# A fused attention and expert kernel: second batch's loads at another place in the queue, and a new order of its steps

## The chip, the cores and the metric

The kernel runs on one core of one Trainium2 chip. The metric is device time in microseconds (us) of one execution; lower is better. The engines are PE (TensorE matmul; PEld is its weight load), DVE (VectorE), ACT (ScalarE), POOL (GpSimd) and SP (SyncE, which here only issues DMAs). Each engine works through its own instructions in program order and waits where an operand isn't there yet.

## What is computed

Four batches, four heads, 1088 positions of 32 values; everything is float32 outside.

```python
a, b = S1 @ x, S2 @ x                    # two sketches of 8 values, for x = q and x = k
phi(x) = outer(a, b)                     # 64 features
kv = sum_s phi(k)_s v_s ;  z = sum_s phi(k)_s
attn = (phi(q) kv) / (phi(q) z + 1e-6)   # 4352 tokens x 128
h = attn @ w_in                          # 128 -> 2048
P = a0 + a1 h + a2 h^2 + a3 h^3 ;  Q = 1 + |b0||h| + |b1| h^2
out = (P / (Q + 1e-6)) @ w_out           # 2048 -> 128
```

## The kernel before

**Stages.** `keys(b)` makes one batch's k features and sums them with v (transposes L414/L416 on DVE, sketches L434 on PE, copies L439 on ACT, features L442 on DVE, products L453 on PE, L470 keeps the sum). `queries(b)` makes q features and the quotient, in chunks of up to 384 positions: transposes L493; then either "direct" (sketches L515, copies L520/L523, features L527/L530; the first 512 positions of batch 0) or "spread" (sketches L543, copy L548, two stores of the sketch to DRAM, `put`, and three reads of it back in a repeated layout, `get`, then features L551); then products L581, L590 to L597 on DVE, transpose back L603 on PE, and L610 on ACT into `xT`. `unit(i)`, 29 of them, takes blocks of 128 hidden values by 256 or 512 tokens: hidden matmuls L683, evacuation L687, |h| L698, L703/L705, L708, Ln L711, Exp L714, L718/L720 and so on, and output matmuls L779 whose weights are w_out times a0..a3 (`w_part`, L390 to L396). A unit's mode (2, 3 or 4) says how the polynomial is split: mode 3 has three output matmuls per block and two products on DVE; mode 2 has two, and instead a product (L732), an addition (L736 on DVE or L738 on ACT) and a product (L741).

**The order.** The program is a list of 976 steps. `step(...)` makes a step in the order in which the code creates it (that index is the step number used below), `PLACE[number]` is its place in the program, and `run` issues all steps by place. `after` and `behind` serve for an assertion on places alone; what really waits for what follows from the data. `rank`, `slack`, `early`, `rate`, `cost` are left from the planner that made PLACE and have no effect when the kernel is built. `ON_ACT` lists the steps, among those that either engine can do, that go to ACT; the others go to DVE. `FILLS` puts matmuls on idle data (L320) ahead of a place.

**Buffers.** `kq` 3 (k or q of one batch), `v_sb` 1, `a_all`, `b_all`, `sk_d` 2 each, PSUM `h` 2, `out` 2, `att` 2.

**Loads.** All go through SP's queue, except k of batch 0 (step 2) and the two tiny loads of `ab_row` (steps 7, 8, the polynomial's constants), which ACT issues first of all. `load_v` is two DMAs: partitions 0 to 63 and 64 to 127. A product L453 contracts over all 128 partitions, so it reads both; the `after` at L464 named both only for the last part.

Steps around the change:

| step | engine | what |
|---|---|---|
| 3 | ACT | preload of the table set (L293) |
| 9, 11 | SP | the halves of w_in |
| 12, 117 | SP | k and q of batch 1 |
| 115, 116 | SP | v of batch 1, first and second half |
| 13, 14 | SP | the halves of w_out |
| 16, 21 | PE | transpose of the sketch matrices L348; bias matmul L376, which spreads `ab_row` |
| 24 to 33 | ACT or DVE | scaled w_out, two halves for each of five versions |
| 71, 87 | ACT | copies L520 and L548 of batch 0, positions 256 to 512 and 512 to 768 |
| 73, 79 | PE | products L581 of positions 256 to 512 |
| 88, 89; 90 to 92 | SP | stores and reads of the first spread chunk (batch 0, 512 to 768) |
| 93, 98, 99 | DVE, PE, ACT | its features L551, transpose back L603, copy L610 |
| 103, 104; 105 to 107 | SP | stores and reads of the second spread chunk |
| 122, 123 | DVE, PE | features L442 and products L453 of batch 1, first part |
| 133 | DVE | transposes L493 of batch 1's first queries |
| 306; 342, 343 | PE; ACT, DVE | first hidden matmul (unit 0); steps of unit 2 (L720, L732) |

Of the kernel before, what the change touches and what calls it, by code (L numbers as in the profile page):

```python
# [20 lines left out]
def kernel(  # L21
# [16 lines left out]
    R = S1.shape[0]  # L38
# [6 lines left out]
    NT = 8  # L45
# [79 lines left out]
    def d_four(n, ptr):  # L125
# [14 lines left out]
    LOADS = 1.3  # L140
    LATER = 4.5
# [4 lines left out]
    GET_SLACK = 0.8  # L146
# [6 lines left out]
    MODES = '43242333333243333233444244434'  # L153
# [12 lines left out]
        0, 3, 1, 39, 4, 5, 6, 2, 20, 19, 9, 28, 25, 11, 18, 7, 8, 12, 16, 15, 13, 42, 43, 76, 57, 72, 56,  # L166
        95, 96, 65, 58, 77, 73, 75, 10, 24, 14, 23, 31, 37, 21, 22, 32, 40, 33, 35, 36, 46, 34, 38, 41, 50,
        44, 48, 49, 51, 53, 17, 29, 26, 30, 54, 55, 60, 62, 67, 68, 69, 45, 52, 66, 61, 70, 71, 78, 85, 91,
        115, 121, 86, 87, 93, 94, 124, 125, 47, 59, 63, 64, 79, 80, 81, 90, 126, 131, 138, 143, 144, 149,
        150, 84, 97, 104, 112, 107, 113, 128, 161, 196, 214, 215, 217, 222, 234, 237, 106, 114, 27, 83, 82,  # L170
        110, 111, 120, 146, 127, 137, 145, 152, 98, 100, 108, 172, 198, 102, 155, 156, 159, 160, 171, 178,
        175, 213, 223, 224, 231, 233, 238, 239, 174, 185, 189, 190, 205, 218, 206, 210, 250, 252, 257, 263,
        272, 283, 284, 165, 201, 202, 211, 212, 227, 261, 228, 262, 279, 280, 301, 316, 330, 346, 298, 311,
        334, 268, 318, 299, 359, 360, 361, 381, 357, 358, 366, 382, 331, 332, 342, 384, 386, 288, 295, 309,
        312, 310, 338, 336, 340, 380, 403, 405, 407, 426, 427, 428, 282, 321, 322, 335, 326, 343, 344, 337,
        388, 394, 408, 411, 429, 458, 459, 300, 374, 385, 396, 397, 400, 436, 399, 437, 445, 456, 466, 471,
        478, 481, 469, 505, 542, 440, 470, 482, 496, 504, 520, 587, 495, 545, 562, 590, 558, 571, 594, 602,
        613, 467, 474, 480, 497, 487, 537, 543, 501, 606, 616, 621, 623, 631, 634, 637, 477, 525, 552, 554,
        553, 563, 611, 609, 647, 659, 675, 677, 682, 692, 693, 568, 575, 577, 585, 584, 684, 586, 610, 685,
        698, 735, 738, 747, 757, 772, 74, 88, 92, 101, 103, 109, 119, 122, 129, 141, 135, 133, 134, 142, 89,  # L180
        105, 116, 117, 132, 139, 140, 157, 123, 173, 181, 184, 270, 264, 99, 136, 147, 148, 154, 162, 163,
        176, 153, 164, 167, 183, 203, 200, 118, 130, 151, 166, 169, 179, 180, 187, 188, 216, 245, 240, 207,
        293, 302, 398, 369, 313, 303, 158, 170, 177, 186, 168, 182, 192, 193, 197, 209, 225, 247, 191, 204,
        219, 251, 269, 305, 241, 296, 333, 278, 194, 199, 220, 221, 195, 208, 226, 232, 235, 243, 256, 266,
        248, 290, 304, 319, 323, 294, 291, 392, 383, 414, 422, 391, 230, 242, 229, 236, 244, 246, 254, 259,
        274, 277, 292, 324, 258, 339, 353, 307, 347, 348, 368, 350, 376, 418, 404, 433, 453, 506, 486, 488,
        541, 249, 253, 255, 260, 265, 267, 273, 281, 289, 315, 328, 354, 271, 371, 379, 417, 349, 364, 413,
        416, 377, 483, 412, 449, 275, 276, 287, 297, 285, 286, 308, 317, 329, 351, 367, 372, 378, 395, 424,
        508, 421, 415, 393, 420, 419, 461, 432, 473, 306, 314, 345, 355, 320, 327, 356, 365, 389, 401, 410,
        431, 425, 441, 447, 512, 489, 490, 513, 515, 556, 485, 491, 465, 529, 538, 536, 535, 534, 532, 530,  # L190
        531, 533, 352, 362, 363, 370, 373, 375, 406, 409, 430, 438, 448, 463, 387, 500, 510, 576, 588, 589,
        511, 549, 547, 517, 526, 527, 390, 402, 325, 341, 423, 434, 439, 444, 452, 462, 479, 507, 457, 499,
        524, 540, 548, 523, 555, 550, 559, 573, 600, 716, 746, 727, 612, 435, 443, 451, 455, 442, 446, 468,
        476, 484, 493, 544, 561, 567, 578, 560, 632, 665, 619, 628, 620, 582, 583, 618, 629, 625, 603, 460,
        472, 464, 475, 450, 454, 498, 521, 546, 564, 566, 579, 503, 595, 626, 580, 591, 581, 641, 593, 636,
        696, 681, 688, 494, 514, 492, 502, 509, 518, 522, 551, 569, 597, 605, 615, 519, 633, 644, 650, 642,
        630, 624, 658, 635, 657, 651, 652, 708, 718, 743, 744, 748, 715, 717, 726, 745, 528, 565, 516, 539,
        557, 570, 599, 604, 607, 617, 627, 639, 596, 649, 668, 706, 725, 689, 753, 671, 729, 730, 719, 775,
        572, 574, 601, 614, 592, 598, 622, 646, 661, 663, 672, 687, 643, 701, 711, 709, 723, 691, 731, 713,
        710, 732, 728, 739, 608, 640, 638, 648, 645, 653, 655, 669, 678, 683, 700, 704, 654, 667, 676, 724,  # L200
        754, 769, 755, 776, 795, 793, 786, 787, 849, 844, 855, 664, 670, 656, 662, 660, 666, 679, 686, 694,
        707, 721, 741, 736, 751, 760, 833, 835, 802, 794, 749, 784, 779, 768, 780, 695, 697, 673, 674, 680,
        690, 702, 712, 734, 750, 765, 767, 763, 788, 791, 832, 818, 817, 799, 778, 785, 800, 801, 819, 841,
        859, 858, 852, 854, 853, 842, 850, 845, 699, 703, 705, 720, 714, 722, 737, 756, 761, 773, 782, 797,
        803, 814, 862, 866, 820, 836, 816, 828, 811, 821, 812, 871, 831, 867, 740, 759, 752, 758, 733, 742,
        762, 766, 789, 805, 806, 813, 838, 847, 827, 822, 829, 863, 843, 869, 896, 868, 890, 870, 877, 889,
        764, 771, 770, 774, 790, 798, 809, 810, 826, 864, 879, 898, 840, 872, 876, 894, 904, 891, 911, 908,
        914, 954, 915, 937, 953, 777, 781, 783, 796, 808, 815, 830, 839, 851, 865, 825, 875, 883, 886, 885,
        922, 909, 905, 804, 807, 792, 823, 824, 837, 860, 861, 880, 895, 899, 906, 892, 893, 924, 913, 926,
        910, 923, 921, 936, 941, 939, 940, 938, 834, 846, 848, 857, 873, 874, 884, 888, 900, 912, 929, 949,  # L210
        931, 934, 925, 927, 933, 946, 965, 950, 878, 881, 887, 897, 901, 907, 916, 928, 951, 955, 942, 943,
        957, 963, 902, 903, 919, 920, 932, 944, 945, 952, 930, 959, 967, 956, 962, 968, 856, 882, 917, 918,
        935, 947, 948, 958, 960, 969, 961, 964, 966, 970, 971, 975, 972, 973, 974,
    )
    ON_ACT = (
        26, 27, 28, 29, 31, 33, 328, 342, 379, 454, 478, 502, 535, 612, 636, 669, 693, 717, 744, 876, 914,
        932, 946, 951, 960,
    )
    FILLS = {8: 15, 14: 4}
# [53 lines left out]
    def load_k(b, buf, rank, after=(), early=0.0, slack=0.3, behind=None, rate=250, eng=SP):  # L273
        return [dma(lambda: buf.t, flat(k, b), rank, 0.557, after, [buf], eng=eng, rate=rate, early=early, slack=slack, behind=behind)]
# [11 lines left out]
    def load_s(i, rank, eng):  # L286
        s_in = (S1, S2)[i]
        return dma(s_raw[i * R:(i + 1) * R], s_in, rank, 0.001, eng=eng, cost=0.4, slack=S_SLACK[i])

    s_l = [load_s(0, -206, SP), load_s(1, -205.9, SP)]  # L290
# [11 lines left out]
    def load_w(x, rank):  # L302
        c = x * 1024
        w_l[x] = dma(w_in_sb[:, c:c + 1024], moe_w_in[:, c:c + 1024], rank, 0.524, early=LATER, rate=440, slack=0.3, behind=v0_l[1])
# [5 lines left out]
    k1_l = load_k(1, k1, K1L_RANK, early=LATER, slack=0.3, behind=v0_l[1], rate=350)  # L310
# [95 lines left out]
    def keys(b, kb, vb, k_l, v_l, rank, parts, wide, early=0.0):  # L406
# [16 lines left out]
        for x, (t0, t1) in enumerate(parts):  # L423
# [40 lines left out]
            last = step(PE, 0.265 * n + 0.07, products, r, after=[ft] + (v_l if t1 > NT else v_l[:1]), uses=[k_p, vb, kv], behind=last)  # L464
# [349 lines left out]
    for b in range(1, B):  # L814
        kb, vb, qb = k1 if b == 1 else Buf("kq"), Buf("v_sb"), Buf("kq")
        base = where(b * S)
        gate = wo_l if b == 1 else q_done[b - 1][-1:]
        kl = k1_l if b == 1 else load_k(b, kb, base - 14, gate, slack=1.0)
        vl = load_v(b, vb, LOADS - 0.01 if b == 1 else base - 13.9, gate, slack=V_SLACK)
        ql = dma(lambda qb=qb: qb.t, flat(q, b), LOADS if b == 1 else base - 13.8, 0.557, gate, [qb], rate=250, slack=V_SLACK)  # L820
        keys(b, kb, vb, kl, vl, max(K1_RANK, base - K_LEAD), ((0, 3), (3, 6), (6, 9)), False, LATE)
        for c0 in range(0, S, QN):
            queries(b, qb, ql, c0, min(c0 + QN, S), max(0.5, where(b * S + c0) - Q_LEAD), "spread")
# [34 lines left out]
```

## Time and profile before

| | us |
|---|---|
| median of 3 runs | 269.05 (268.74 to 269.28) |
| the profiled execution | 268.98 |
| its span | 267.2 |
| PE busy | 257.3 (96%) |
| DVE busy | 252.7 (95%) |
| ACT busy | 248.2 (93%) |
| POOL busy | 2.7 (1%) |
| DMA moved | 20.13 MB, mean 75 GB/s |

Times inside the profile count from the start of the span; some 1.8 us of the execution lie around it. Busy time is the union of an engine's instructions. SPq and ACTq are the engines' DMA issues, a "releaser" is what the profile takes to have ended a wait, inferred from semaphores; where the named engine had long been done, it was another.

### The profile page before, as it was taken

Reading aid. Unit: us, or ns where it says so; the run is one execution under the profiler, and the core shown is the slowest. Engines: PE = TensorE matmul, PEld = TensorE weight load, DVE = VectorE, ACT = ScalarE, POOL = GpSimd, SP = SyncE. Lnnn points to the kernel's source line nnn. Section 1 sums busy time; section 2 is a strip of 40 time slices with the busy share of each in tenths; the row PEclk is TensorE's granted clock in tenths of the full one; section 3 lists DMA queues with packets and bytes.
Section 4 is the critical chain, followed back from the end, with each engine's and each line's share of the span. In section 5 each row is a group of like instructions: output and inputs, shape, how many; then the busy total and the mean of one; then the engine's idle time right before and its main releaser. Section 6 shows DMA issues by size and latency. Waiting matters only on the chain.

```text
span 267.2 us, 4218 instructions
## 1 busy us (share of the span) xinstructions
PE 257.3 (96%) x1660; PEld 140.9 (53%) x1660; DVE 252.7 (95%) x294; ACT 248.2 (93%) x208; POOL 2.7 (1%) x25
## 2 busy tenths in 40 slices
PE   8989699999999999999999999999999999999993
PEld 5767545554545455444534445454544466465782
DVE  3989789999999999999999999999999999999994
ACT  1699699999999999999999999999999999999990
POOL 4000000000000000000000000000000000000000
PEclk9999999999999999999999999999999999999999
DMA  7954433660024825300135515000022000013013
GB/s 204 313 226 132 119 98 103 166 207 0 2 56 101 168 55 151 121 0 11 36 70 105 150 40 132 12 2 0 0 29 39 2 10 0 0 27 45 0 27 54
DMA packets 29063, 20.13 MB, mean 75 GB/s; under 512 B 19316, under 2 KB 24948, under 8 KB 29044
## 3 DMA queue, kind: packets, MB, share of 16 engines
q1 hardware_dynamic: 28352, 19.24, 28.4%
q10 hardware_dynamic: 692, 0.62, 0.8%
q8 instruction: 13, 0.21, 0.3%
q14 instruction: 6, 0.05, 0.1%
HBM read 16.65 MB, written 3.21 MB: 74 GB/s over the span
## 4 chain that ended last, share of the span: by engine, by line
PE 32%; DVE 29%; ACT 25%; issue 11%; DMA 1%; SPq 0%; DVEq 0%; ACTq 0%
PE h_ps L683 16%; ACT ln L711 7%; PE out_ps L779 6%; ACT t L687 6%; DVE t L726 5%; ACT t L714 5%; DVE t L723 5%; ACT t L720 4%; DVE t L708 4%; DVE t L698 3%; DVE t L729 3%; PE att_ps L453 3%; DVE t L703 2%; DVE t L744 2%; PE att_ps L581 2%
## 5 line engine op out<-in xcount | busy, mean ns | idle before, releaser
L683 PE MATMUL h_ps<-xT,w_in_sb 128*128 128x512 f32 (+1 forms) x320 | 128.3, 534 | 0.4
L779 PE MATMUL out_ps<-t,w_out 128*128 128x512 bf16 (+1 forms) x501 | 101.3, 345 | 0.3 <-DVE t L726 0.2
L683 PEld LDWEIGHTS h_ps<-xT,w_in_sb 128*128 128x128 f32 x320 | 58.7, 190 | 42.4 <-issue 32.1
L779 PEld LDWEIGHTS <-w_out 128*128 128x128 bf16 x501 | 47.6, 98 | 51.3 <-issue 19.8
L687 ACT CAST t<-h_ps 128x1024 bf16<-128x1024 f32 (+1 forms) x69 | 69.2, 1027 | 0.7 <-PE h_ps L683 0.6
L711 ACT ACTIVATE ln<-t 128x3072 f32<-128x3072 bf16 (+4 forms) x29 | 65.0, 2240 | 0.1
L714 ACT ACTIVATE t<-ln 128x3072 bf16<-128x3072 f32 (+4 forms) x29 | 64.7, 2231 | 0.3
L723 DVE TENSOR_TENSOR t<-t,t 128x3072 bf16<-128x3072 bf16 (+4 forms) x29 | 40.4, 1395 | 0.0
L708 DVE TENSOR_TENSOR t<-t,t 128x3072 bf16<-128x3072 bf16 (+4 forms) x29 | 40.3, 1393 | 0.0
L720 ACT ACTIVATE t<-t,a_sb 128x3072 bf16<-128x3072 bf16 (+3 forms) x15 | 38.3, 2552 | 0.1
L726 DVE TENSOR_TENSOR t<-t,t 128x3072 bf16<-128x3072 bf16 (+4 forms) x24 | 33.3, 1392 | 0.0
L703 DVE TENSOR_SCALAR t<-t,b_abs 128x3072 bf16<-128x3072 bf16 (+2 forms) x25 | 23.8, 951 | 0.1
L698 DVE TENSOR_SCALAR t<-t 128x3072 uint16<-128x3072 uint16 (+4 forms) x29 | 22.4, 775 | 0.9 <-ACT t L687 0.9
L729 DVE TENSOR_TENSOR t<-t,t 128x3072 bf16<-128x3072 bf16 (+2 forms) x14 | 22.1, 1575 | 0.0
L581 PEld LDWEIGHTS att_ps<-kvz,a_all 128*64 128x64 f32 x288 | 9.5, 137 | 6.7 <-issue 3.7
L581 PE MATMUL att_ps<-kvz,a_all 128*64 128x66 f32 x288 | 11.3, 226 | 0.6 <-DVE a_all L527 0.5
L744 DVE TENSOR_TENSOR t<-t,t 128x1024 bf16<-128x1024 bf16 (+3 forms) x10 | 11.1, 1115 | 0.0
L453 PE MATMUL att_ps<-v_sb,k_p 128*64 128x64 f32 x216 | 8.0, 225 | 2.5 <-DVE t L708 2.5
L453 PEld LDWEIGHTS att_ps<-v_sb,k_p 128*64 128x64 f32 x216 | 7.0, 137 | 6.2 <-DVE t L708 2.8
L551 DVE TENSOR_TENSOR a_all<-a_all,b_all 128x768 f32<-128x768 f32 (+2 forms) x11 | 9.6, 877 | 0.0
L732 DVE TENSOR_TENSOR t<-t,t 128x3072 bf16<-128x3072 bf16 (+2 forms) x5 | 7.2, 1432 | 2.4 <-ACT t L720 2.4
L442 DVE TENSOR_TENSOR k_p<-att_ps,b_sk 128x768 f32<-128x768 f32 x9 | 8.6, 951 | 0.3 <-ACT b_sk L439 0.3
(74 smaller groups left out, 136.8 us busy)
## 6 DMA issues: line engine op xcount, KB each, us to landing
a_all<-sk_d SPq DMA_DIRECT2D x6, 384.0 KB
b_all<-sk_d SPq DMA_DIRECT2D x12, 192.0 KB
kq<-in_k_dram SPq DMA_DIRECT2D x3, 544.0 KB
kq<-in_q_dram SPq DMA_DIRECT2D x3, 544.0 KB
a_all<-sk_d SPq DMA_DIRECT2D x4, 320.0 KB
b_all<-sk_d SPq DMA_DIRECT2D x8, 160.0 KB
v_sb<-in_v_dram SPq DMA_DIRECT2D x4, 288.0 KB
v_sb<-in_v_dram SPq DMA_DIRECT2D x4, 256.0 KB
```

The source lines that it names most:

```text
L683: nc.tensor.matmul(h.t[:, cols[x] - cols[x0]:cols[x + 1] - cols[x0]], lhsT=w_in_sb[:, f * 128:(f + 1) * 128], rhs=xT[:, xpos(t0):xpos(t0) ...
L687: nc.scalar.copy(out=hh.t[:, cols[x0]:cols[x1]], in_=h.t[:, 0:cols[x1] - cols[x0]])
L698: nc.vector.tensor_scalar(out=u.t[:, :n].bitcast(U16), in0=hh.t[:, :n].bitcast(U16), scalar1=0x7FFF, scalar2=None, op0=AX.bitwise_and)
L703: nc.vector.tensor_scalar(out=w.t[:, :n], in0=u.t[:, :n], scalar1=ab1, scalar2=ab0, op0=AX.mult, op1=AX.add)
L708: nc.vector.tensor_mul(out=y.t[:, :n], in0=w.t[:, :n], in1=u.t[:, :n])
L711: nc.scalar.activation(out=ln.t[:, :n], in_=y.t[:, :n], func=ACT.Ln, bias=1.0 + 1e-6)
L714: nc.scalar.activation(out=r.t[:, :n], in_=ln.t[:, :n], func=ACT.Exp, scale=-1.0)
L720: nc.scalar.activation(out=p.t[:, :n], in_=hh.t[:, :n], func=ACT.Identity, scale=a3, bias=a2)
L723: nc.vector.tensor_mul(out=s.t[:, :n], in0=hh.t[:, :n], in1=r.t[:, :n])
L726: nc.vector.tensor_mul(out=(hh if mode == 3 else p).t[:, :n], in0=hh.t[:, :n], in1=s.t[:, :n])
L729: nc.vector.tensor_mul(out=hh.t[:, :n], in0=p.t[:, :n], in1=hh.t[:, :n])
L779: nc.tensor.matmul(o[0].t[:, :bl[x][1]], lhsT=w_sb[y_][:, bl[x][2], :], rhs=src.t[:, cols[x]:cols[x + 1]], start=(o[1] == 1), stop=(o[1] = ...
```

## The change

The code, with the long lists cut:

```diff
-    GET_SLACK = 0.8
+    GET_SLACK = 0.9
...
-    MODES = '43242333333243333233444244434'
+    MODES = '43242333333243333233444244424'
...
-        0, 3, 1, 39, 4, 5, 6, 2, 20, 19, 9, 28, 25, 11, 18, 7, 8, 12, 16, 15, 13, 42, 43, 76, 57, 72, 56,
+        0, 1, 2, 7, 5, 6, 10, 3, 4, 43, 11, 45, 39, 16, 14, 8, 9, 17, 23, 18, 55, 13, 15, 34, 97, 53, 96,
...
-        26, 27, 28, 29, 31, 33, 328, 342, 379, 454, 478, 502, 535, 612, 636, 669, 693, 717, 744, 876, 914,
-        932, 946, 951, 960,
+        27, 28, 29, 30, 32, 342, 351, 379, 454, 478, 502, 535, 612, 636, 669, 688, 693, 744, 878, 889, 914,
+        932, 946, 951, 953,
...
-    FILLS = {8: 15, 14: 4}
+    FILLS = {9: 15, 19: 2}
...
-            last = step(PE, 0.265 * n + 0.07, products, r, after=[ft] + (v_l if t1 > NT else v_l[:1]), uses=[k_p, vb, kv], behind=last)
+            last = step(PE, 0.265 * n + 0.07, products, r, after=[ft] + v_l, uses=[k_p, vb, kv], behind=last)
...
-        vl = load_v(b, vb, LOADS - 0.01 if b == 1 else base - 13.9, gate, slack=V_SLACK)
-        ql = dma(lambda qb=qb: qb.t, flat(q, b), LOADS if b == 1 else base - 13.8, 0.557, gate, [qb], rate=250, slack=V_SLACK)
+        vl = load_v(b, vb, LOADS - 0.01 if b == 1 else base - 13.9, gate, slack=3.0 if b == 1 else V_SLACK, behind=w_l[1] if b == 1 else None)
+        ql = dma(lambda qb=qb: qb.t, flat(q, b), LOADS if b == 1 else base - 13.8, 0.557, gate, [qb], rate=250, slack=2.0 if b == 1 else V_SLACK, behind=vl[1] if b == 1 else None)
```

Three more edits touch `slack`, `early` and `behind` of the loads of s, w_in and k1. Nearly all 976 places differ. Read out by step number, the starts of the queues are:

| queue | before | after |
|---|---|---|
| SP | 0, 1, 4, 5, 6, 10, 13, 14, 9, 12, **117**, 11, 88, 89, 90, 91, 92, **115**, 104, 103, 105, **116**, 106 | 0, 1, 4, 5, 6, 10, 14, 13, 12, 9, 11, 89, 88, **115, 116**, 91, 90, 92, **117**, 104, 103, 107, 105, 106 |
| PE | 16, 36, 40, 59, 58, 44, 48, 39, 43, **21**, 52, 47, 51, 55, 69, 62, 86, 70, 66, 73, 306, 79, 320 | 16, **21**, 36, 40, 58, 59, 44, 48, 52, 39, 43, 47, 51, 55, 69, 86, 62, 70, 66, 79, 73, 306, 128, 77, 320 |
| ACT | 2, 7, 8, 41, 37, 60, 45, 49, **3**, 22, 53, 56, 26, 71, 87, 29, 67, 33, 23, 31, 307 | 2, 7, 8, **3**, 22, 41, 37, 60, 45, 23, 49, 53, 56, 29, 87, 71, 28, 67, 27, 30, 307 |

(36 to 56 are batch 0's keys, 57 to 84 its direct queries, 306, 307 and 320 the first units.) The 15 idle matmuls stay ahead of step 16; ahead of step 36 there are two instead of four.

Work that goes to another engine, or changes:

| step | what | before | after |
|---|---|---|---|
| 26, 31, 33 / 30, 32 | scaled w_out, 1024 each | ACT / DVE | DVE / ACT |
| 328 (unit 1), 351 (unit 3) | L720/L718 and L705/L703, 1024 | ACT, DVE | DVE, ACT |
| 688 (unit 16), 717 (unit 17) | 3072 | DVE, ACT | ACT, DVE |
| 876, 878 (unit 23), 889 (unit 24) | 2048 | ACT, DVE, DVE | DVE, ACT, ACT |
| 960 (unit 28) | 256 | ACT | DVE |
| unit 27 | 768 | mode 3 | mode 2, its addition (953) on ACT |

## Prediction

> **What bounds the kernel.** I read the page's busy shares first: PE 96%, DVE 95%, ACT 93%. Three engines that full cannot be read from an average, so I cut the span into stretches (columns: PE, PEld, DVE, ACT, POOL busy us, then PE's granted clock, the DMA engines' share, GB/s).
>
> ```profile
> 0.00:14.25 14.25, 12.17 (x165) 8.89 (x167) 8.77 (x24) 6.49 (x16) 2.74 (x25) 1.00 0.90 267
> ...
> 28.70:31.20 2.50, 0.02 (x1) 0.00 (x0) 2.46 (x6) 1.41 (x2) 0.00 (x0) 1.00 0.75 170
> 30.15:32.55 2.40, 1.29 (x28) 1.09 (x30) 1.61 (x4) 0.00 (x0) 0.00 (x0) 1.00 0.20 54
> 31.80:34.10 2.30, 2.30 (x44) 1.63 (x40) 0.00 (x0) 1.52 (x3) 0.00 (x0) 1.00 0.03 7
> 44.00:164.00 120.00, 119.60 (x779) 58.92 (x777) 119.02 (x121) 119.11 (x94) 0.00 (x0) 1.00 0.33 84
> 164.00:243.00 79.00, 79.00 (x347) 40.61 (x344) 78.84 (x71) 78.54 (x51) 0.00 (x0) 1.00 0.11 20
> 243.00:253.50 10.50, 10.50 (x64) 7.36 (x63) 10.50 (x12) 10.50 (x9) 0.00 (x0) 1.00 0.05 7
> ```
>
> From 44 to 253.5 us nothing is free: in 209.5 us PE idles 0.40, DVE 1.14, ACT 1.35. Whatever delays all three before 44 us delays the end by as much. And there is such a place: PE stands still in the 28.70 stretch, ACT in the 30.15 one, DVE in the 31.80 one. The timeline says who follows whom (the bracket is the idle time before the instruction):
>
> ```profile
> 26.53 0.63 SPq L268 DMA_DIRECT2D v_sb<-in_v_dram  x1
> ...
> 31.25 0.92 PE L453 MATMUL att_ps<-v_sb,k_p 128*64 128x64 f32 x24 [2.53 <-DVE t L708]
> 32.10 0.44 PE L603 MATMUL att_ps<-ident,x_tok 128*128 128x128 f32 x2
> 32.58 0.37 ACT L610 COPY xT<-att_ps 128x256 f32<-128x256 f32 x1 [2.44 <-PE att_ps L603]
> 32.84 1.24 ACT L720 ACTIVATE t<-t,a_sb 128x1024 bf16<-128x1024 bf16 x1
> 34.12 0.69 DVE L732 TENSOR_TENSOR t<-t,t 128x1024 bf16<-128x1024 bf16 x1 [2.35 <-ACT t L720]
> ```
>
> PE's first key product of batch 1 (step 123) waits 2.53 us. Its releaser is named DVE L708, but its k_p (step 122) was written at 23.75 to 24.7, and L708 writes a tile it doesn't read. What it does read and what comes last is the second half of v, issued at 26.53: 4.7 us later PE runs. Behind 123 in PE's order stands the transpose back of step 98, behind that ACT's copy (step 99), behind that ACT's step 342, and DVE's step 343 waits for it. One late load thus costs PE 2.53, ACT 2.44, DVE 2.35 us.
>
> **Part 1: both v halves go up SP's queue.** They move from behind 92 and 105 to right behind the first two sketch stores. In before these stores run at 14.13 to 15.33, and SP then waits until 18.85 for them to land. Two v issues of 0.65 us fit into that gap and cost SP nothing. The only v_sb buffer is free: batch 0's products end at 11.6. By the 4.7 us from issue to use they land at 21 at the latest, and 123's turn on PE comes after 26.8. The stall goes: PE -2.53, ACT -2.44, DVE -2.35. Next latest for 123 would be k_p, ready before. The sketch reads (90 to 92) now have v's 0.56 MB ahead of them; they feed DVE's step 93, which ran at 25.32. Cost taken 0, since q1's bytes (below) no longer stand ahead of the stores; if that cover fails, v's bytes at 379 GB/s (the 14.25 to 17.20 stretch) cost 1.4 us.
>
> **Part 2: q1 moves back, the w_in halves with it.** q1 (step 117) was issued at 9.86, goes behind 92, so to 20.8 us at the latest (where the reads are all issued in before), and by the same 4.7 us lands by 25.5; its first reader, 133, is now DVE's 53rd step instead of its 35th, and DVE's 53rd ran at 30.5 in before, 28 without the stall. Hidden. The first w_in half now goes behind k1. Bytes count here: 14.25 us at 267 GB/s is 3.80 MB, exactly s, k0, q0, v0, w_out, one w_in half and k1. So the half that had passed after 3.25 MB passes at 14.25 instead of about 12.6, and its reader (step 306) starts after 15.94. Margin 1.7 us, cost 0. The second half passes earlier, since q1 is gone from ahead of it.
>
> **Part 3: the head's order.** PE's bias matmul (21) goes from 9.59 to directly behind step 16, ahead of all sketches. It needs ab_row. The DMA view of 4 to 9 us shows one packet on ACT's queue, at 4.1:
>
> ```profile
> q10 hardware_dynamic: 1, 0.00, 0.0%
> ```
>
> k0's packets on that queue ended before 4.0 and its reader ran at 4.62, so I put ab_row at 4.2 plus up to 1.1, about 5.2. PE is at 5.10 then; 0.38 for the bias matmul (row L376) and 0.52 for two fills (four take 1.03) give 6.0 to 6.2 for the first sketches, 6.00 before. Cost 0 to 0.2 if so; by rows alone ab_row may land anywhere between 4.1 and its first use at 9.59, which would cost up to 4 us (a rival below). I take 0.1.
> After the keys (last feature of L442 at 11.1 both ways, as L530 merely goes ahead of three L442), ACT copies 87 (0.27) before 71, and PE does both products 79 and 73 (0.46 each) before the first hidden matmul. That starts 0.7 later, 0.46 of it only moved: +0.27 on PE.
> The table preload (step 3) moves to the start of ACT's work. Before, ACT loads twice, 1.28 us each, at 2.00 and 8.94; copies, casts, Abs, Ln and Exp after the second need no third, so one load goes. It lay in ACT's slack (next copy's input comes at 10.24), so it gains 0. The Trainium skill (ScalarE: Activation LUTs, What ACT_TABLE_LOAD costs) gives 1283 ns for the load and about 1380 ns of drain. The load agrees; the drain does not show, ACT's copy starts at 10.24, 0.02 after the load's end. By its 2.66 us ACT would gain 2.66 in the head, and the end still nothing.
>
> **Part 4: work moved between engines.** Rows: weight 1.15 ACT or 0.74 DVE; L720 or L705 at 1024 1.25 or 1.23, at 2048 2.1, at 256 0.60; on DVE 0.53, 0.8 and 0.3. Head: one weight and step 328 from ACT to DVE, 351 the other way: ACT -1.17, DVE +0.7. Late: 688 and 717 cancel, 876 and 878 cancel; 889 puts 2.1 on ACT, unit 27's mode 1.0, step 960 takes 0.6 off: ACT +2.5, DVE -0.4. Unit 27 loses three matmuls on PE, 0.3.
>
> **Sum, per engine.** PE -2.53 + 0.27 + 0.1 = -2.2 (the 0.3 at the end not counted). DVE -2.35 + 0.7 - 0.4 = -2.05. ACT -2.44 - 1.17 + 2.5 = -1.1, but ACT's last instruction ends at 260.56 and DVE's at 263.73, so it has 3.2 us spare. The least of the two that set the end: **-2.0 us**. The profiled execution took 268.98 (span 267.2 and 1.8 around it), 0.07 below the median of 269.05. So 267.0 for it, and 267.0 (267.05) by the median. Own range: 1.3 gained if the head's unknowns go wrong (0.2 for ab_row, 0.5 of short waits) to 3.0 if the small waits shrink too: 266.0 to 267.8. All of parts 1 to 4 is in a list of 976 places rewritten as a whole; what it does to the body has no row, from below 0 (at most the 0.4 to 1.4 us that the body idles) to whatever waits it brings.
>
> **Rivals.**
> *ACT becomes the bound late.* For: in the chain of waits ACT already carries 243 to 253.5 us, and +2.5 us falls just before. If the 1.17 saved early is only waited away, ACT nets 0: 269.1; if it counts, 267.9. I take 268.5. Against: the 3.2 us spare. Chance 0.12.
> *The stall moves to step 93*: sketch reads behind v, the 1.4 us of part 1, 268.4. Against: SP can't issue the reads before the stores land, and v drains meanwhile. 0.05.
> *PE waits at the bias matmul (slower).* Place: PE's second instruction; everything PE does stands behind it. Price: one us for each us that ab_row lands after 5.3, at most 4.3: 271.3. It decides from 7.3 on (gain gone), slower by 0.2% from 7.9 on. For: first use at 9.59 proves no earlier. Against: its packet went at 4.1. 0.07. PE's granted clock stayed 1.00 through the 2.5 us of idle in the 28.70 stretch. The Trainium skill (TensorE: Matmul & The Clock Gate, What's actually happening) lets it fall to half after an idle window of some 3.4 us, which agrees, and only in this rival could PE idle so long: an estimate from that page is 1.7 us more (3.4 us of work at half rate).
> *The rewritten body brings waits of its own.* Full engines have nothing to absorb them. One wait as long as the one removed gives 269.5; two of 1 us 269.0; three of 1.2 us 270.6. From 2.6 us on it is slower. Against: the DMA-to-reader distances in the new list look like the old ones. 0.18.
>
> **Chances.** Forecast 0.58. Some 0.2% (0.54 us) is what a measurement of this kernel can tell from no change, so faster is below 268.5, slower above 269.6. Faster: 0.58 + 0.05 + half of ACT's 0.12 + 0.05 of the body's = 0.74. Same: 0.06 + 0.05 = 0.11. Slower: 0.07 + 0.08 = 0.15. The range that leaves out no more than 2 in 10: 265.9 to 269.6.
>
> **What would show it.** Right: L453 of batch 1 without idle before it, v_sb issued by 17 us, no idle of 2 us on any engine between 17 and 44, one table load, hidden matmuls of unit 4 (33.65 before) at about 31.7. Wrong: idle before L376 near 5 us or before step 93 near 24; ACT without idle and DVE waiting for it after 220 us; PE, DVE and ACT idle summing to more than before between 44 and 253.5.

## The result, and the profile after

| | before | after |
|---|---|---|
| median of 14 executions each (us) | 270.48 (268.74 to 273.07) | 266.3 (265.78 to 268.75) |
| ratio | | 0.9879, 95% interval 0.984 to 0.9917 |
| profiled execution, its span (us) | 268.98, 267.2 | 266.81, 265.0 |
| PE, DVE, ACT busy (us) | 257.3, 252.7, 248.2 | 254.6, 253.2, 247.9 |

By the ratio the change is faster by 1.2%; the two medians alone would give 1.5% (0.9846). The median of before was 269.05 over three executions and is 270.48 over 14, because many of its executions run at a lower mean clock of PE (see the end of the experiments). Between the two profiled executions the gain is 2.2 us.

First the stretches of the changed kernel (columns as before: PE, PEld, DVE, ACT, POOL busy, PE's clock, DMA share, GB/s):

```profile
0.00:14.25 14.25, 12.07 (x165) 8.67 (x165) 9.15 (x24) 5.01 (x15) 2.75 (x25) 1.00 0.92 257
14.25:17.20 2.95, 2.15 (x22) 1.63 (x23) 2.92 (x11) 2.95 (x5) 0.00 (x0) 1.00 0.87 297
17.20:44.00 26.80, 26.17 (x239) 16.28 (x238) 24.97 (x47) 25.17 (x34) 0.00 (x0) 1.00 0.60 133
44.00:164.00 120.00, 118.67 (x752) 59.80 (x761) 119.20 (x121) 119.51 (x90) 0.00 (x0) 1.00 0.38 87
164.00:243.00 79.00, 77.64 (x333) 41.04 (x339) 78.93 (x69) 78.81 (x52) 0.00 (x0) 1.00 0.09 14
243.00:253.50 10.50, 10.30 (x67) 7.01 (x66) 10.47 (x15) 10.47 (x9) 0.00 (x0) 1.00 0.10 15
```

From 17.2 to 44 us PE idles 0.63, DVE 1.83 and ACT 1.63 us; before, the same stretch held 24.12, 23.44 and 23.70 us of work, so 2.68, 3.36 and 3.10 us of idle time. From 44 to 253.5 us DVE idles 0.90 (1.14 before) and ACT 0.71 (1.35): the body was full and is full. PE's 2.89 there (0.40 before) is probably not idle time. The profile's page has 498 weight loads of the output matmuls (L780) but only 480 matmuls; 18 records are missing, and where a record is missing PE looks idle (an estimate: one such matmul adds 0.2 us of busy time, 18 add 3.7).

The stall is gone. The first fence is SP's queue, the second the timeline behind it:

```profile
13.54 1.20 SPq L268 DMA_DIRECT2D sk_d<-sk_sb  x2
14.84 1.36 SPq L268 DMA_DIRECT2D v_sb<-in_v_dram  x2
19.20 0.65 SPq L268 DMA_DIRECT2D b_all<-sk_d  x1
```

```profile
25.78 0.69 DVE L552 TENSOR_TENSOR a_all<-a_all,b_all 128x512 f32<-128x512 f32 x1 [0.96 <-DMA b_all<-sk_d]
...
26.62 0.69 PE L582 MATMUL att_ps<-kvz,a_all 128*64 128x66 f32 x16 [0.63 <-ACT t L721]
...
27.78 1.62 PE L454 MATMUL att_ps<-v_sb,k_p 128*64 128x64 f32 x48
...
29.81 0.37 ACT L611 COPY xT<-att_ps 128x256 f32<-128x256 f32 x1 [0.27 <-PE att_ps L604]
...
31.57 1.98 PE L684 MATMUL h_ps<-xT,w_in_sb 128*128 128x512 f32 x4
```

Both halves of v are issued by 16.2 us, and the products of batch 1 (L454, L453 before) have no bracket: PE does not wait. The copy behind them waits 0.27 us where it waited 2.44. Unit 4's hidden matmuls start at 31.57, 2.08 us earlier than the 33.65 of before. This nearly accounts for the 2.2 us of the span: the gain is complete by 32 us. A new wait is there too: DVE's step 93 waits 0.96 us for the sketch to come back from DRAM.

### The profile page after: what moved, and what is told of

Its sections match the earlier page's. It is cut to its first block, busy times and chain, and to the rows that moved or that the text cites. A ratio compares the mean times of both kernels' runs of the same rounds, so it can differ in the third digit from the quotient of the medians.

```text
span 265.0 us, 4193 instructions
## 1 busy us (share of the span) xinstructions
PE 254.6 (96%) x1637; PEld 140.8 (53%) x1655; DVE 253.2 (96%) x295; ACT 247.9 (94%) x207; POOL 2.8 (1%) x25
## 4 chain that ended last, share of the span: by engine, by line
PE 38%; DVE 34%; issue 9%; DMA 8%; ACT 6%; SPq 2%; DVEq 0%; ACTq 0%
PE h_ps L684 21%; PE out_ps L780 12%; DVE t L724 8%; DVE t L709 5%; DVE t L727 5%; DVE t L704 4%; DVE t L699 3%; SPq L268 2%; DMA w_in_sb<-in_moe_w_in_dram 2%; DMA b_all<-sk_d 2%; PE att_ps L582 2%; DVE t L730 2%; ACT t L688 2%; DMA kq<-in_q_dram 2%; ACT ln L712 1%
## 5 line engine op out<-in xcount | busy, mean ns | idle before, releaser
L780 PE MATMUL out_ps<-t,w_out 128*128 128x512 bf16 (+1 forms) x480 | 98.8, 344 | 1.7 <-issue 0.6
L780 PEld LDWEIGHTS <-w_out 128*128 128x128 bf16 x498 | 47.5, 98 | 51.1 <-issue 20.6
L688 ACT CAST t<-h_ps 128x1024 bf16<-128x1024 f32 (+1 forms) x69 | 68.4, 1020 | 1.2 <-PE h_ps L684 1.0
L709 DVE TENSOR_TENSOR t<-t,t 128x3072 bf16<-128x3072 bf16 (+4 forms) x29 | 40.3, 1397 | 0.1
L724 DVE TENSOR_TENSOR t<-t,t 128x3072 bf16<-128x3072 bf16 (+4 forms) x29 | 40.3, 1396 | 0.0
L727 DVE TENSOR_TENSOR t<-t,t 128x3072 bf16<-128x3072 bf16 (+3 forms) x23 | 32.8, 1430 | 0.0
L721 ACT ACTIVATE t<-t,a_sb 128x3072 bf16<-128x3072 bf16 (+2 forms) x12 | 32.0, 2668 | 0.1
L730 DVE TENSOR_TENSOR t<-t,t 128x3072 bf16<-128x3072 bf16 (+1 forms) x13 | 21.6, 1664 | 0.0
L704 DVE TENSOR_SCALAR t<-t,b_abs 128x3072 bf16<-128x3072 bf16 (+3 forms) x23 | 21.6, 938 | 0.0
L706 ACT ACTIVATE t<-t,b_abs 128x1024 bf16<-128x1024 bf16 (+3 forms) x6 | 10.6, 1773 | 0.0
L733 DVE TENSOR_TENSOR t<-t,t 128x3072 bf16<-128x3072 bf16 (+3 forms) x6 | 7.7, 1281 | 0.0
L742 DVE TENSOR_TENSOR t<-t,t 128x3072 bf16<-128x3072 bf16 (+3 forms) x6 | 7.7, 1280 | 0.0
```

What stands on the lines that cost most here:

```text
L688: nc.scalar.copy(out=hh.t[:, cols[x0]:cols[x1]], in_=h.t[:, 0:cols[x1] - cols[x0]])
L704: nc.vector.tensor_scalar(out=w.t[:, :n], in0=u.t[:, :n], scalar1=ab1, scalar2=ab0, op0=AX.mult, op1=AX.add)
L709: nc.vector.tensor_mul(out=y.t[:, :n], in0=w.t[:, :n], in1=u.t[:, :n])
L721: nc.scalar.activation(out=p.t[:, :n], in_=hh.t[:, :n], func=ACT.Identity, scale=a3, bias=a2)
L724: nc.vector.tensor_mul(out=s.t[:, :n], in0=hh.t[:, :n], in1=r.t[:, :n])
L727: nc.vector.tensor_mul(out=(hh if mode == 3 else p).t[:, :n], in0=hh.t[:, :n], in1=s.t[:, :n])
```

## The experiments

All were timed in five rounds, beside runs of the kernel before on the same chip. Line numbers shift by up to four against before where lines were added.

**1. Part 1 alone** (b_v), in the kernel before:

```diff
+    PLACE = list(PLACE)
+    PLACE[115], PLACE[116] = 79.1, 79.2
```

> The kernel before with one thing changed: both v halves of batch 1 (steps 115, 116) go right behind the first two sketch stores, all else stays. My theory (the late second half of v is the whole gain): the idle of 2.53, 2.44 and 2.35 us ahead of L453, L610 and L732 goes, and the time falls by 2.3 us, to a ratio of about 0.991; a new wait of up to 1 us may show ahead of the first L551, since v's bytes stand ahead of the sketch reads. Rival (the new order as a whole brings the gain, and the stall would have been made up for): the stall goes in the profile, but the span falls by less than 0.7 us.

Measured: 266.86 us (266.42 to 267.2), ratio 0.9874 (0.9846 to 0.9901). Two moved DMAs give all that the whole change gives. Foreseen were 2.3 us; by the medians it is 3.5, and why it is more stands at the end of the experiments. Two views of this kernel, the timeline and a stretch:

```profile
25.28 0.68 DVE L553 TENSOR_TENSOR a_all<-a_all,b_all 128x512 f32<-128x512 f32 x1
...
28.61 0.92 PE L455 MATMUL att_ps<-v_sb,k_p 128*64 128x64 f32 x24
...
31.01 3.70 PE L685 MATMUL h_ps<-xT,w_in_sb 128*128 128x512 f32 x8
```

```profile
17.20:44.00 26.80, 26.65 (x238) 17.00 (x238) 25.94 (x48) 26.11 (x35) 0.00 (x0) 1.00 0.41 113
```

Here too the products have no bracket, unit 4 comes 2.64 us earlier than before, and step 93 does not wait, although v's bytes are ahead of its reads: SP issues these at 19.76 instead of 18.85, and DVE needs them at 25.28. The margin is thin: in the profile of b_v_fill2 (point 4), which has the same two moves, SP issues the reads at 20.61 and step 93 waits 0.54 us.

**2. The stall put back** into the changed kernel (a_v_late): v behind the reads again, its second half behind the first read of the second chunk (step 107), and q's `behind` dropped.

```diff
+    PLACE = list(PLACE)
+    PLACE[115], PLACE[107], PLACE[116] = 90.5, 117.4, 117.6
...
-        ql = dma(..., slack=2.0 if b == 1 else V_SLACK, behind=vl[1] if b == 1 else None)
+        ql = dma(..., slack=2.0 if b == 1 else V_SLACK)
```

> The changed kernel with part 1 undone: the first half of v behind the three reads of the first chunk, the second half behind one read of the second chunk (107), as in the kernel before. My theory: SP issues the second half at about 28.0 us, it can be used 4.7 us later, at 32.7, and L453 had its turn at 27.8, so PE stalls 4.9 us and the time grows by 4 to 5 us over the changed kernel. Rival (the new order brings the gain and can absorb a late v): less than 1 us more than the changed kernel.

Measured: 274.54 us (272.16 to 274.78), ratio 1.0141 (1.0101 to 1.0181), slower than before. The late half was issued at 29.02, and the stall is longer than it ever was:

```profile
29.02 0.80 SPq L270 DMA_DIRECT2D v_sb<-in_v_dram  x1
...
34.32 2.83 PE L456 MATMUL att_ps<-v_sb,k_p 128*64 128x64 f32 x48 [4.52 <-DVE t L711]
...
37.72 0.37 ACT L613 COPY xT<-att_ps 128x256 f32<-128x256 f32 x1 [5.53 <-PE att_ps L606]
...
39.26 0.69 DVE L711 TENSOR_TENSOR t<-t,t 128x1024 bf16<-128x1024 bf16 x1 [5.61 <-ACT t L708]
```

The same 48 products take 2.83 us here and 1.62 without the stall. The stretches of this kernel say why (third column from the end: PE's granted clock):

```profile
30.00:34.00 4.00, 0.00 (x0) 0.00 (x0) 3.65 (x8) 2.15 (x3) 0.00 (x0) 1.00 0.89 186
34.00:36.00 2.00, 1.68 (x32) 1.71 (x34) 0.00 (x0) 0.00 (x0) 0.00 (x0) 0.51 0.34 85
36.00:38.00 2.00, 2.00 (x36) 1.65 (x35) 0.00 (x0) 0.28 (x2) 0.00 (x0) 0.64 0.00 0
```

After 4.5 us of idle time PE gets half its clock, in the trace's record of the clock from 34.04 to 37.45 us, and then the full one again. So the size was missed: 4 to 5 us over the change were foreseen, and the medians differ by 8.2. A stall of this length is paid twice, once waiting and once at half rate: 4.5 us and, by estimate, 1.7 us for 3.4 us at half clock, together 6.2. The remaining 2 us or so belong to the second group of times of point 4, in which this profiled execution lies (274.70, 6.2 above the change's second group, 268.55); in how many of the others it is so is not known. From issue to use it is 5.3 us here, against 4.7 in before.

**3. Where the reads and q stand.** One kernel puts v behind the reads of the first chunk (a_v_reads), one puts q ahead of the stores again, here behind the second half of w_in (a_q_early, `behind` dropped as in 2).

```diff
+    PLACE = list(PLACE)
+    PLACE[115], PLACE[116] = 90.1, 90.2
```

> The changed kernel with both v halves two steps of the queue later: behind the three reads of the first chunk, still ahead of q1. Theory (v's bytes hold up the stores and reads, which cost 0.96 us ahead of the first L551): the stores land about 1 us sooner, the wait ahead of L551 goes, v can be used at about 26 us, ahead of its turn at 27.8, and the time falls by 0 to 0.9 us. Rival (the reads are slow by themselves, or q1's bytes make them so): the wait ahead of L551 stays at 1 us, the time within 0.3 us; if v lands past 27.8, L453 waits instead and the time grows.

```diff
+    PLACE = list(PLACE)
+    PLACE[117] = 45.1
```

> The changed kernel with part 2 undone as to q1: step 117 goes directly behind the second half of w_in, ahead of the sketch stores. Theory (stores, v and reads queue behind each other by bytes): 0.557 MB at some 390 GB/s land 1.4 us ahead of the stores, the reads of the first chunk start about 1.4 us later, the wait ahead of the first L551 grows from 0.96 to about 2.4 us and the time by 0.5 to 1.4 us. Rival (the stores' landing doesn't depend on what is queued ahead): the wait ahead of L551 stays at 1 us or shrinks, since q1 no longer shares the queue with the reads, and the time stays within 0.3 us.

Measured: 268.5 us (267.14 to 268.93), ratio 0.9932 (0.9904 to 0.996), and 268.16 us (266.44 to 268.94), ratio 0.9915 (0.988 to 0.9949). Neither is better than the change, and the gain expected of a_v_reads did not come. Its wait at step 93 is gone, but only because DVE reaches that step later: it runs at 25.68, in the change at 25.78. The stores landed hardly sooner: the first read, which waits for them, is issued at 18.93, with the stores at 13.53; in the change at 19.20, with the stores at 13.54; and in experiment 6, where v also stands ahead, at 17.93 with the stores at 13.54. These 1.3 us are not explained by v's bytes. The traces show 16 landings for each of these loads and stores, and in the three profiles SP issues the first read 0.07 or 0.08 us behind the last landing of the second store. 13 of its 16 landings lie between 16.1 and 17.0 us in all three profiles, but the last at 19.12 in the change, 18.85 in a_v_reads and 17.86 in experiment 6. Why the last ones lag is open. What a_v_reads lost in its profiled execution stands elsewhere:

```profile
17.27 1.99 PE L686 MATMUL h_ps<-xT,w_in_sb 128*128 128x256 f32 x8 [0.97 <-DMA w_in_sb<-in_moe_w_in_dram]
```

Unit 0 waits for the first half of w_in. The profile of a_q_early is of the second kind of point 4 and can't show what was expected of step 93; its three shortest times (266.44 to 266.64) are some 0.6 us above the change's. Six of the seven times of a_v_reads lie at 268.26 to 268.93 and four of the eight of a_q_early at 268.67 to 268.94, and that leads to the next point.

**4. Two groups of times.** Of the 14 executions of the change nine took 265.78 to 266.81 us and five 268.3 to 268.75, with nothing between. The kernel with part 1 alone has no second group. The profiles of a_v_late, a_q_early and a_889 (5) happened to fall in a head (the first 14 us) like that of the second fence, whose lines are of a_fill4 (below); the first fence is the change's own:

```profile
5.47 0.39 PE L321 MATMUL h_ps<-idle 128*128 128x256 bf16 x2
5.80 0.69 PE L435 MATMUL h_ps<-S,kT 128*64 128x64 f32 x16
...
9.31 2.32 PE L454 MATMUL out_ps<-v_sb,k_p 128*64 128x64 f32 x72
```

```profile
5.41 1.03 PE L321 MATMUL h_ps<-idle 128*128 128x256 bf16 x4
6.38 1.12 PE L435 MATMUL h_ps<-S,kT 128*64 128x64 f32 x16
...
11.65 3.22 PE L454 MATMUL out_ps<-v_sb,k_p 128*64 128x64 f32 x72
```

The same 16 sketches take 0.69 or 1.12 us and the 72 products 2.32 or 3.22: in the second case PE works at a lower rate from 5 to beyond 11 us, and unit 0 starts at 19.26 instead of 16.33 (18.72 in a_889, which has two idle matmuls like the change). The column of the granted clock shows 1.00 in both, but it counts time ahead of the clock's first record as 1.00. That record, at full clock, begins at 5.42 us in the trace of the change and at 13.73 in that of a_fill4, and there the pace changes: in a_fill4 two products start every 107 ns before it and every 58 ns behind it. In the four profiles of the second kind it begins at 13.01 to 13.73 us, in the ten others at 4.16 to 6.62. So the second group is PE at about half its rate until 13 us or later, a slow head. What holds it there is the question. First guess: the change has two idle matmuls fewer ahead of the sketches, so PE is not warm. Two kernels, the change with four and part 1 alone with two:

```diff
-    FILLS = {9: 15, 19: 2}
+    FILLS = {9: 15, 19: 4}
```

> The changed kernel with four idle matmuls instead of two ahead of the first sketches (step 36). The changed kernel's times fall in two groups, 265.8 to 266.8 and 268.3 to 268.8 us. Theory (in the upper group PE's clock is still at half while the keys of batch 0 are made: 16 sketch matmuls take 1.12 us there against 0.69; two idle matmuls too few to set it free in every execution): the upper group goes, all times lie between 265.7 and 267.0 us, 0.1 to 0.4 us above the lower group of the changed kernel for the two more matmuls. Rival (the two groups have another cause, such as the landing of the first loads): some runs stay near 268.5 us.

```diff
-    FILLS = {8: 15, 14: 4}
+    FILLS = {8: 15, 14: 2}
```

> The kernel before with part 1 alone, whose six times lay between 266.4 and 267.2 us, and two idle matmuls instead of four ahead of the first sketches. Theory (too few idle matmuls leave PE's clock at half in some executions): a second group of times appears 2 to 3 us above the first, as in the changed kernel. Rival (it needs the bias matmul in front too, or has another cause): one group, at 266 to 267 us.

Measured: a_fill4 266.09, 266.62, 268.71, 268.96, 269.03 and 269.13, four of six in the upper group, ratio 0.9885 (0.9827 to 0.9943); b_v_fill2 266.44 to 267.86, ratio 0.986 (0.9816 to 0.9903), no upper group. That theory falls in both kernels: the number of idle matmuls does not decide.

**5. One piece of late work back to DVE** (a_889):

```diff
-        ..., 688, 693, 744, 878, 889, 914,
+        ..., 688, 693, 744, 878, 914,
```

> The changed kernel with step 889 (unit 24, 128x2048) on DVE again instead of ACT; ACT loses 2.1 us of work late, DVE gains 0.8 us. Theory of my sum (DVE and PE set the end, ACT has spare): the time grows by 0.3 to 0.8 us in each group. Rival (ACT is the bound late): the time falls by up to 1 us.

Measured: 266.41, 266.47, 266.67, 266.89, 267.14 and one of 269.22; ratio 0.9857 (0.9807 to 0.9906). The lower group's median is 266.67, that of a_bias_late (6, same chip) 266.21 and that of the change 265.94, so the piece is worth some 0.5 to 0.7 us on ACT. ACT is not the bound.

**6. The bias matmul back behind the products** (a_bias_late):

```diff
+    PLACE = list(PLACE)
+    PLACE[21], PLACE[22], PLACE[23] = 42.5, 42.6, 42.7
```

> The changed kernel with the bias matmul (21) and its two ACT copies (22, 23) back behind the second key product, as in the kernel before; part 3 undone as to this. My prediction gave the early place a cost of 0.1 us: so the time of each group falls by 0 to 0.3 us. Rival (the bias matmul's wait for ab_row opens a hole that leaves PE's clock at half): the upper group of times becomes rarer or goes. A third reading (it fills a hole, as the idle matmuls do): the upper group becomes more frequent.

Measured: 265.86, 265.93, 266.21, 266.24, 266.57 and one of 269.07; median 266.22, ratio 0.9839 (0.9787 to 0.989). The lower group does not move down, and one in six against 5 in 14 does not yet say that the upper one is rarer. So the bias matmul was then moved by itself, in the kernel with part 1 alone, where no upper group had been seen (step 8, a load that ACT issues, only keeps its place ahead of it); and in the change the first direct sketches were put in their old order, alone and with the late bias matmul:

```diff
+    PLACE[8], PLACE[21] = 2.5, 8.5
```

> The kernel before with part 1 (v behind the first two sketch stores) and with the bias matmul ahead of all sketches, as the change has it; nothing else. Theory 'the early bias matmul, which waits or works on one row in PE's first microseconds, is what lets the slow head happen': besides times of 266.4 to 267.2 a second group near 268.5 to 269 appears, in at least 2 of 6 executions. Rival 'it needs the changed order of the first direct sketches': all executions within 266.3 to 267.9, as without the bias matmul moved.

```diff
+    PLACE[59], PLACE[58], PLACE[60] = 25, 30, 30.5
```

> The changed kernel with the first two direct sketches in the old order (59 ahead of 58), bias matmul still early. Theory 'the early bias matmul lets the slow head happen': two groups stay, 265.8 to 266.8 and 268.3 to 269, with at least 2 of 6 in the upper. Rival 'the order of the sketches': one group, 265.8 to 266.8.

> The changed kernel with both in the old order: bias matmul late, sketches 59 ahead of 58. By either theory the slow head is gone: all executions 265.7 to 266.8.

| kernel | bias matmul | sketches | times (us) | of them above 268.2 |
|---|---|---|---|---|
| b_v, b_v_fill2 | late | old order | 266.42 to 267.86 | 0 of 12 |
| b_v_bias | early | old order | 266.62 to 266.95, 268.62 to 268.81 | 5 of 12 |
| after | early | new order | 265.78 to 266.81, 268.3 to 268.75 | 5 of 14 |
| a_q_early, a_fill4, a_889 | early | new order | 266.09 to 267.66, 268.67 to 269.22 | 9 of 20 |
| a_bias_late, a_bl_win (7) | late | new order | 265.86 to 266.57, 269.05 to 269.07 | 2 of 12 |
| a_swap | early | old order | 265.77 to 266.98 | 0 of 6 |
| a_bl_swap | late | old order | 266.09 to 267.79 | 0 of 6 |

Ratios: b_v_bias 0.9908 (0.9875 to 0.994), a_swap 0.9861 (0.9819 to 0.9902), a_bl_swap 0.9882 (0.9839 to 0.9926). Of a_bl_swap all times were expected below 266.8; three of six are longer, without reaching the upper group.

The early bias matmul makes the second group more frequent. In the kernel with part 1 it is the one thing moved (0 of 12 against 5 of 12, which an exact test gives 1 time in 50 by chance), and over the whole table it is 2 of 30 without and 19 of 52 with it. It is not the only condition: the group also came up twice with the bias matmul late, and not in six executions of a_swap with it early, though at 19 in 52 six such come up 1 time in 15 by chance.

The other condition seems to be when the clock can change. The records at full clock are 252.59, 256.00 or 259.41 us long, so they differ by steps of 3.41 us, and the steps fall differently in each execution. In the four profiles of the second kind a step fell at 6.18 to 6.90 us and did not free the clock, nor did the next; all four have the early bias matmul in the 3.41 us before that step. In before and b_v, without it, a step fell at 6.62 and did. In the eight others the clock was freed at 4.16 to 5.42. That the two together decide is argued from these profiles, not shown; none of them has the second kind of head with the bias matmul late.

**7. The first w_in half ahead of k again**, with the late bias matmul (a_bl_win):

```diff
+    PLACE[21], PLACE[22], PLACE[23] = 42.5, 42.6, 42.7
+    PLACE[12], PLACE[9] = 43, 39
```

> The changed kernel with the bias matmul where it was (behind the first products) and the first w_in half ahead of k of batch 1, as before. If unit 0's first hidden matmul really waits for that half, it starts up to 0.4 us earlier (16.33 in the profile of the change) and the time falls by 0.1 to 0.4 from the 266.2 of the late bias matmul alone. Rival 'the products ahead of it end at that time anyway': no difference, 266.0 to 266.4.

Measured: 265.95, 266.01, 266.02, 266.23, 266.25 and 269.05; ratio 0.987 (0.982 to 0.992). Against 265.86 to 266.57 (and one of 269.07) without it that is no difference: unit 0 starts at 16.13 with it and 16.05 without. No version was clearly better than the change's lower group.

**Why the medians gained more than the stall.** The stall was 2.35 us long on DVE, but the medians differ by 3.3 (0.9879 of 270.48) to 4.2 us. Each timed execution comes with PE's mean granted clock. Of 42 executions of the kernel before beside the experiments, 15 had a clock of 0.994 to 0.999 and took 268.37 to 269.65 us, and 27 had 0.985 to 0.993 and took 270.14 to 272.65. Of b_v, b_v_fill2, b_v_bias and the change none was below 0.996. Against the 15 (median 269.15) part 1 alone (266.86) gains 2.3 us: the stall. The rest of the medians' difference belongs to executions in which the clock was lower. One record at half clock as in a_v_late, 3.41 us long, lowers the mean over an execution by 0.006; by that estimate 22 of the 27 (0.990 to 0.993, median 270.63) hold one more than the 15, and five (0.985 to 0.987, from 271.31 on) two. Only the kernels with a wait of PE near 2 us or more show such clocks (a_v_late 0.978 to 0.994; three executions of a_bl_swap, at 0.993 or 0.994 and 267.35 to 267.79 us; its profiled execution has PE waiting 1.80 us near 15 us). That a stall is followed by a lower clock was seen in a trace only in a_v_late; for before it is a conclusion from times and clocks, and from b_v, where v is the only thing moved and none of six executions has such a clock.

## Why the prediction was right

The forecast was 267.0 us, the profiled execution took 266.81 and the median is 266.3. Point by point:

- **Part 1, the stall: right.** Foreseen were -2.53, -2.44 and -2.35 us; alone it moved unit 4 by 2.64 and the median by 2.3 against executions of before at a like clock. The chain "v, products, transpose back, ACT's copy, then DVE" held: put back into the changed kernel, where other steps stand behind the copy, the wait goes through PE (4.52), ACT (5.53) and DVE (5.61 us).
- **Part 1, the reads behind v at no cost: right in b_v** (issued 0.91 us later and hidden), not in every execution (0.54 us in b_v_fill2). The rival "the stall moves to step 93" saw the place of a new wait: in the change's profile the step waits 0.96 us, of which 0.46 us is a later start (25.78 against 25.32) and 0.5 us that DVE came earlier. Its reason, v's bytes, is not what the runs show: the issue of the reads varies by 1.3 us with v ahead in both cases (experiment 3).
- **Part 2: right in the end, wrong in a term.** q is hidden. But the first half of w_in was said to pass at 14.25 with 1.7 us to spare. In the chain of waits of the changed kernel it lands just as unit 0 begins (the first line is its issue and the time to landing):

```profile
9.98 6.30 DMA w_in_sb<-in_moe_w_in_dram
16.28 0.04 issue
16.33 1.99 PE h_ps L684 x8
```

  The margin was nothing. The step "the half passes when the bytes ahead of it have" gives the landing of its first part, not of its last: the 16 landings of this half lie between 12.74 and 14.45 us in before, where 12.6 was assumed, and between 14.60 and 16.28 in the change, where 14.25 was. The shift by k1's bytes was sized well (1.65 foreseen, 1.83 at the last part); the spread of some 1.7 us was left out. It cost nothing on the median (experiment 7) because what PE does ahead of unit 0 ends at that time too, though a_v_reads and a_swap waited for it (0.97 and 0.30 us).
- **Part 3, the head: right for most executions, and the step that failed.** The bias matmul did not wait for ab_row (4.98 us, no bracket; the rival is false), the sketches began at 5.80 instead of 6.0 to 6.2, and unit 0 at 16.33, 0.39 later than before (0.1 + 0.27 was foreseen). But "cost 0.1" counted only when the sketches start, not at which rate PE runs behind them. In 5 of 14 executions the head costs 2.6 us more; in the traces of such heads the clock is freed only after 13 us. Against part 1 alone the rest of the change wins some 0.9 us in nine executions (265.94 against 266.86) and loses some 1.7 in five (268.55): about nothing on the whole, as the two ratios 0.9879 and 0.9874 say.
- **The table load: right.** One load, at 2.03, and ACT has 2.26 us of idle time behind it.
- **Part 4: right.** ACT's last instruction ends at 259.53 and DVE's at 261.55; ACT's end moved by 1.03 us (1.1 foreseen), 2.0 of the 3.2 us are still spare, and the rival "ACT becomes the bound" did not come. The single piece that was taken back was worth 0.5 to 0.7 us.
- **The body brings no waits** on DVE and ACT (0.90 and 0.71 us, less than before).
- **The sum** was -2.0; DVE's end moved by 2.18 us (263.73 to 261.55). That the time fits so well is partly luck, twice over. The rest of the change adds nothing to the sum only because its gains and its slow heads cancel. And the sum was taken off 269.05, from three executions of before that all took as long as those at the higher clock; over 14 the medians differ by 4.2 us, and some 1.3 of them (270.48 against 269.15) are the lower clock behind the stall, a cost that the prediction did not have.

The Trainium skill (TensorE: Matmul & The Clock Gate, What's actually happening) describes a gate that halves PE's clock after an idle window of about 3.4 us, frees it after a busy one, and runs free, so that the moment differs from run to run. Experiment 2 agrees in size (0.51 after 4.5 us, a record of 3.41 us at half clock), and the two heads agree with its run-to-run difference. That a busy window frees the clock did not show in the four slow heads: PE was busy for 3.2 to 3.3 of the 3.41 us ahead of the step at 6.18 to 6.90 us, and the lower rate stayed for 6.8 us more.

## What to carry to other kernels

When three engines are full in the body, look for the one load whose late arrival stops all three in turn, and move its issue, not the work: two DMAs put into a gap in which the queue waits anyway gave the whole gain here, and all the other new places gave nothing that the ratios show. Count a PE stall of several microseconds twice, for the wait and for the clock behind it, and compare executions at like clocks before comparing with the stall's length. Look at single times, not only the median: a reordering of the first microseconds can cost 2.6 us in a third of the executions and leave the median where it is. Where a view shows full clock, compare the durations of equal matmuls before believing it.

## What the runs showed that was not expected

- A 4.5 us wait of PE was followed by 3.4 us at half its granted clock (0.51 and 0.64 in two stretches of 2 us; 48 products: 2.83 instead of 1.62 us).
- The same head runs in two ways, 2.6 us apart, from execution to execution; the durations show it (16 sketches: 0.69 or 1.12 us) and so does the start of the clock's first record (4.16 to 6.62 or 13.01 to 13.73 us), but the column of the granted clock does not (1.00 in the stretch).
- Two stores of a sketch to DRAM issued at 13.54 us let the first read be issued at 17.93 us in one profile and at 19.20 in another; 13 of the 16 landings of the second store come at like times, the last 1.3 us apart.
- The bytes ahead of a load and a mean rate give its first landing, not its last: 14.25 foreseen, 14.60 the first of 16 and 16.28 the last.
